# Other durations in a kernel's planner, narrower mask matmuls in the first batch, and rotating tiles handed out by the planner

## Chip, cores, metric

One core of a Trainium2 chip. The metric is the device time of one execution in microseconds; the median of three runs stands for the kernel. A profile of one further execution, with a start and a duration for each instruction, is what the numbers below are read from.

## What is computed

Block-sparse causal attention over four batches of eight heads (768 tokens, head size 64), and then a two-layer feed-forward block with a tanh GELU on the 3072 resulting tokens. In the attention each query sees its own block of 64 keys and those blocks whose mean key scores in the top three.

```python
gate_scores = einsum('bhsd,bhnd->bhsn', q, k.reshape(B,H,12,64,D).mean(3))   # causal blocks only
top_idx = argsort(gate_scores)[..., -3:]
mask = blocks(top_idx | own_block) & causal
attn = softmax(where(mask, 0.125 * q @ k.T, -1e9))
x = (attn @ v).transpose(0, 2, 1, 3).reshape(3072, 512)
out = gelu_tanh(x @ w_in) @ w_out          # 512 -> 2048 -> 512
```

A query in the first three blocks (rows 0 to 191) has at most three causal blocks, so all of them are chosen.

## The kernel before

The work is cut into 16 head pairs `p` (four per batch `b`; `hp` is the place in the batch) and, per batch, a first layer `s1(b)` and a second layer `s2` (`s2_plain(0)` for the first batch; in `s2(b)` of the others 7 half-size products per token tile, with sums formed on VectorE, take the place of 8). While one batch is in its feed-forward part, the pairs of the next are prepared.

**A planner sets the order.** Nothing is issued where it is written. Each piece of work is an `Op` with the engines that it may run on and a duration for each (`add({DVE: 0.56, ACT: 0.84}, ...)` may go to either), the ops that it waits for, a priority, and the buffers it takes and gives back. `Plan.solve` (L53) simulates the engines: of the ops that could start within 0.03 us of the earliest it takes the one with the lowest priority number, and books it on the engine where it would end first. When all are placed, they are issued in order of their planned start (L1226 to L1229). So the given durations decide three things: the order on each engine, which engine gets an op that two could do, and which pooled buffer an op gets. On the chip each engine runs its instructions strictly in the order issued, waiting on semaphores where an input is late: a wrong duration costs only if it makes something early wait behind something late.

**Fillers.** `warm` (L1163) adds 72 matmuls (`NWARM`) of 256 columns at the lowest priority (1e6), whose results nobody reads. The planner puts them wherever it believes TensorE idle, in their order, until they are used up.

**One pair of batch 0** (`pre`, `first` branch): keys and queries are turned by TensorE (`turn`, L391), copied out of PSUM, and the block gate (L512) is a small fp32 matmul; VectorE picks the top three (`sel_e`, L546); TensorE transposes the mask (`mask`, L586). Then `heads2` (L674) goes through six units per pair. For a unit `st_e` (L683) writes the scores of two heads into one of two 1024-column PSUM tiles (`wide`): for each block of columns two matmuls, one per head, of keys by queries, and two that add the mask (`E2` by `mT2`). ScalarE takes exp (`ex_e`, L702), GpSimd cuts the diagonal (`af_e`), TensorE multiplies by the values (`pv_e`, L748), VectorE normalises (`norm2`), TensorE turns the result back (`ot_e`, L808).

**One pair of batches 1 to 3** (`pre`, other branch): VectorE turns keys and queries (`tr`, L414, 0.97 us each) and sums the keys of each block (`ks_all`, L458); the halves are cast to fp16 by VectorE or GpSimd (`kc_all`, L465) and by VectorE or ScalarE (`q16`, L578); gate and choice as above; the mask rows are copied under the queries (`mc`, L627), so that one matmul does scores and mask together (`heads`, L845).

**The feed-forward stage.** `s1(b)` writes 16 units of 8 matmuls into the same two `wide` tiles, each emptied by one GELU on ScalarE (`ge_e`, L949). `s2_plain(0)` is 6 tiles of 16 matmuls, interleaved by the planner with batch 1's attention; each tile is copied out by `cp_e` (L1036) on VectorE or ScalarE. `sums` (L998) and `w_sums` (L980) are the VectorE sums for the later second layers.

**Tiles.** PSUM tiles are pooled by the planner (`takes`, `gives`). Most rotating tiles in the other memory come from pools of the framework, which turn in the order in which the tiles are asked for at issue: loads (`io`, 3 buffers per kind, `iov`, 2), `hd` (3), `hd2` (2), `atp` (6), `obp` (2). In the planner the load buffers are represented by dependences (`free_sd`), others by `last`.

Loads of batches 1 to 3 go out on SyncE's queue in 128-byte rows (`emit_t`, L258); the queue also carries the output stores, in the planned order.

Of the kernel before, what the change touches and what calls it, by code (L numbers as in the profile page):

```python
# [8 lines left out]
FP32 = mybir.dt.float32  # L9
# [123 lines left out]
def kernel(  # L133
# [22 lines left out]
    HALF = S // 2  # L156
    FAST = range(1, B)
# [6 lines left out]
    io = ctx.enter_context(tc.tile_pool(name="io", bufs=PF))  # L164
    iov = ctx.enter_context(tc.tile_pool(name="iov", bufs=PV))
    hd = ctx.enter_context(tc.tile_pool(name="hd", bufs=3))
    hd2 = ctx.enter_context(tc.tile_pool(name="hd2", bufs=2))
    atp = ctx.enter_context(tc.tile_pool(name="atp", bufs=6))
    xtp = ctx.enter_context(tc.tile_pool(name="xtp", bufs=2))
    obp = ctx.enter_context(tc.tile_pool(name="obp", bufs=2))  # L170
# [17 lines left out]

    w_in16 = persist.tile([128, HP, DFF], FP16)
# [23 lines left out]
    for i in range(NB):  # L213
# [8 lines left out]
        "at": ([[x] for x in range(6)], 6), "osb": ([[x] for x in range(2)], 2),  # L222
# [20 lines left out]
    free_sd = {}  # L243

    def load(p, key, held=None, prio=None):
        b, hp = divmod(p, HP)

        def emit(_):
            sd = room.pop(0) if b == 0 and room else (
                iov if key == "v" else io).tile(  # L250
                [128, NC, 2, 64], FP32, tag=key, name=f"{key}_sd_{p}")
            for hh in range(2):
                nc.sync.dma_start(
                    out=sd[:, :, hh, :],
                    in_=SRC[key][b, 2 * hp + hh].rearrange(
                        "(c p) d -> p c d", p=128))
            T[key, p] = sd
        def emit_t(_):  # L258

            sd = io.tile([128, NC * 4, 32], FP32, tag=key, name=f"{key}_sd_{p}")  # L260
            for hh in range(2):
                for a in range(2):
# [7 lines left out]
                 [free_sd.get((key, p - (PV if key == "v" else PF)))  # L270
                  if p - (PV if key == "v" else PF) >= HP else None, held]
                 + moved[-2:-1],
                 prio=10 * p if prio is None else prio)
# [25 lines left out]
    def cast_v(p, old):  # L299
        b, hp = divmod(p, HP)  # L300

        def emit(eng):
            copy(eng, v16[p % NB][:, :, :, 0:64], T["v", p])
        free_sd["v", p] = ld["v16", p] = add(
            {POOL: 0.85}, emit,
            [ld["v", p], old],
            prio=1000 * (b - 1) + 599 + hp if b else 100 * hp - 55)
# [74 lines left out]
    def pre(p):  # L382
# [5 lines left out]
        kcs, ksr, qcs = [], [], []  # L388
        ks = ks16[p % NK]
# [24 lines left out]
        def tr(key):  # L414
            def emit(_):
                T[key + "T32", p] = (hd if key == "q" else hd2).tile(
                    [128, S], FP32, tag=key + "T32", name=f"{key}T32_{p}")
# [5 lines left out]
        if first:  # L423
            for a in range(2):
                t = add({PE: 0.72}, turn("k", a),
                        [ld["k", p] if p else ld["k", 0, a]], pr,
                        takes=("pre", ("wk", p, a)))
                kc = add({DVE: 0.55},
# [3 lines left out]
                def ksb_h(_, a=a):  # L432
                    for x in ([ksb3[p % NK]] if p else
# [11 lines left out]
                        [t, last.get(p - NK, {}).get("gate")], pr - 0.1)  # L445
# [3 lines left out]
                if a == 1:  # L449
                    free_sd["k", p] = t  # L450
            T["ksb", p] = ksb3[p % NK]
        else:
            t = add({DVE: 0.98}, tr("k"),
                    [ld["k", p], last.get(p - 2, {}).get("k32"), sel_3[0]],
                    pr)
            free_sd["k", p] = t
# [6 lines left out]
            ksr.append(add({DVE: 0.93}, ks_all, [t], pr))  # L463
# [9 lines left out]
        def ksb_m(_):  # L473
# [7 lines left out]
                   ksr + [last.get(p - NK, {}).get("gate")], pr))  # L481

        last.setdefault(p, {})["k32"] = add({"NONE": 0.0}, lambda _: None,
                                            kcs + ksr, pr)

        if first:
            def q32():
                if ("qT32", p) not in T:
                    T["qT32", p] = hd.tile([128, S], FP32, tag="qT32",
                                           name=f"qT32_{p}")  # L490
                return T["qT32", p]
            for a in range(2):
                t = add({PE: 0.37}, turn("q", a),
                        [ld["q", p] if p else ld["q", 0, a]], pr,
                        takes=("pre", ("wq", p, a)))
                if a == 1:
                    free_sd["q", p] = t
                qcs.append(add({DVE: 0.55, ACT: 0.49}, turned("q", a, q32),
                               [t, last.get(p - 3, {}).get("pre")], pr,
                               gives=[("wq", p, a)]))  # L500
        else:
            t = add({DVE: 0.98}, tr("q"),
                    [ld["q", p], last.get(p - 3, {}).get("pre")], pr)
            free_sd["q", p] = t
# [4 lines left out]
        for a, (lo, hi) in enumerate(parts):  # L509
# [18 lines left out]
            last.setdefault(p, {})["gate"] = g  # L528

            def gm_e(_, a=a, lo=lo, hi=hi, n=n):  # L530
                if a == 0:
                    T["gx", p] = hd2.tile([128, NC - 1, 32], FP32, tag="gx",
                                          name=f"gx_{p}")
                    T["gm", p] = hd2.tile([128, NC - 1, 2, NBLK], FP32,
                                          tag="gm", name=f"gm_{p}")
                    T["mx8", p] = hd2.tile([128, NG, 8], FP32, tag="mx8",
                                           name=f"mx8_{p}")
                    T["sel", p] = hd2.tile([128, NG, NBLK], FP32, tag="sel",
                                           name=f"sel_{p}")
# [4 lines left out]
                     gives=[("gt", p, a)])  # L544

            def sel_e(_, a=a, lo=lo, hi=hi, n=n):  # L546
# [8 lines left out]
                for x in range(2 * lo, 2 * hi):  # L555
# [9 lines left out]
                      [gx, c_E["gates"], c_E["ones", i]], pr)  # L565
            sels.append(sel)

# [26 lines left out]
        def mask_dma(_):  # L594
            T["mT", p] = hd2.tile([128, S - 128], FP16, tag="mT",
                                 name=f"mT_{p}")
# [4 lines left out]
        if first:  # L601
            mcs = []
            for a, (lo, hi) in enumerate(parts):
                m = add({PE: 0.06 * (hi - lo)},
                        lambda _, a=a, lo=lo, hi=hi: mask(_, a, lo, hi),
                        [sels[a]], pr, takes=("pre", ("mk", p, a)))

# [11 lines left out]
        else:  # L619
# [3 lines left out]
            else:  # L623
                go = add({SP: 1.3}, mask_dma, [sel], -50)
                m = add({"DMA": 0.8}, lambda _: None, [go], pr, lag=6.0)

# [9 lines left out]
            if byPE:  # L636
                add({"NONE": 0.0}, lambda _: None, mcs, pr,
                    gives=[("mk", p, 0)])
            rdy[p] = [kcs[0::2] + [q16s[0], mcs[0], c_E["fill", i]],
                      kcs[1::2] + [q16s[1], mcs[1], c_E["fill", i]]]  # L640
        if p == HP - 1:
            sel_3.append(sel)
        last.setdefault(p, {})["pre"] = add(
            {"NONE": 0.0}, lambda _: None, kcs + q16s + mcs, pr)
# [10 lines left out]
    def table(key, deps, prio):  # L655
        if key not in tables:
            def emit(_):
                t = hd.tile([128, 1], FP32, tag="tab", name="tab_%s_%d" % key)
# [15 lines left out]
    def heads2(p):  # L674
# [3 lines left out]
        for ui, unit in enumerate(units(p)):  # L678
# [4 lines left out]
            def st_e(_, u=u, unit=unit):  # L683
                st = plan.buf[("st",) + u]
                col = 0
                for jc, q0, w in unit:
                    for src, msk in ((kT2[i], False), (E2, True)):
                        mov = mT2[i] if msk else qT2[i]
                        for h in range(2):
                            nc.tensor.matmul(  # L690
                                st[:, 512 * h + col:512 * h + col + w],
                                src[64 * h:64 * h + 64,
                                    jc * 128:jc * 128 + 128],
                                mov[64 * h:64 * h + 64, q0:q0 + w],
                                start=not msk, stop=msk,
# [3 lines left out]
            st = add({PE: n * 2 / 2400 + 0.01}, st_e, rdy[p][late], pr,  # L699
                     takes=("wide", ("st",) + u))  # L700

            def ex_e(_, u=u, n=n):  # L702
                T["at", u] = atp.tile([128, 2, 512], FP16, tag="at",
                                      name="at_%d_%d_%d" % u)
# [5 lines left out]
            ex = add({ACT: 0.17 + 2 * n * 0.000833}, ex_e,  # L710
# [26 lines left out]
            for a in range(2):  # L737
# [21 lines left out]
                pvs[a].append(add({PE: 0.066 * len(cells) + 0.01}, pv_e,  # L759
# [6 lines left out]
        def norm2(a):  # L766
            def emit(_):
                pvv = plan.buf["pv", p, a][:, 0:NC * 66].rearrange(
                    "p (c w) -> p c w", w=66)
                if ("xn", p) not in T:  # L770
                    T["xn", p] = hd.tile([128, NC, 2, 64], FP16, tag="xn",
                                         name=f"xn_{p}")
                zr = hd.tile([128, NC, 1], FP32, tag="zr", name=f"zr_{p}_{a}")
# [7 lines left out]
                     gives=[("pv", p, a)]) for a in range(2)]  # L781
# [478 lines left out]
```

## Time and profile before

| | |
|---|---|
| three runs | 264.86, 265.20, 265.74 us; median 265.2 |
| the profiled execution | 265.39 us, of which 263.7 us from the first to the last instruction |
| TensorE busy, matmuls | 255.0 us (97% of the span) |
| VectorE / ScalarE / GpSimd busy | 180.9 / 162.5 / 83.2 us |
| granted TensorE clock | 0.998 |
| fillers (L1168) | 72, 12.8 us busy |
| first-batch scores (L690) | 192 matmuls |

How to read it: a matmul's recorded duration holds its whole way through the array, while the next one is already fed in. So the time that a stream of matmuls costs is the distance between their starts, and "97% busy" doesn't mean that TensorE ran at its best for 97% of the time. A row of the timeline such as `37.49 0.34 PE L690 ... x2` is a run of two matmuls that began at 37.49 us and whose last result came 0.34 us later. A bracket at the end of a row gives the idle time before it and what ended it.

### The profile page before, as it was taken

The numbers are of one execution on the slowest core, as the hardware profiler recorded it, in microseconds if no ns is written. First come the engines' busy times: TensorE is split into PE (matmuls) and PEld (weight loads), VectorE is DVE, ScalarE is ACT, GpSimd is POOL, SyncE is SP. The second block draws the span as 40 slices with busy tenths as digits, with TensorE's granted clock in tenths as the row PEclk, the third lists the DMA queues.
The fourth block names the chain that finished last, engine by engine and source line by source line (L and its number), as shares of the span: only waits on it lengthen the run. The fifth ranks groups of instructions, "written<-read, shape, count | busy, mean of one in ns | idle before, by whom it ended". The sixth has DMA issues, their size and how long they took to land.

```text
span 263.7 us, 6523 instructions
## 1 busy us (share of the span) xinstructions
PE 255.0 (97%) x2542; PEld 176.8 (67%) x2542; DVE 180.9 (69%) x531; ACT 162.5 (62%) x203; POOL 83.2 (32%) x165
## 2 busy tenths in 40 slices
PE   6999999999998999999989999999999999999994
PEld 5877777565555555555756788665777797666883
DVE  1877745714489999989999999969644463335643
ACT  2368678556968986566887971367799912664000
POOL 8667723002446563221065743100044400000000
PEclk9999999999999999999999999999999999999999
DMA  8998998999798959887896862320104222000222
GB/s 163 218 203 154 159 208 116 176 203 190 155 210 149 206 122 215 173 165 138 154 188 127 160 151 81 104 52 0 27 1 124 50 80 83 0 1 2 80 80 82
DMA packets 130816, 32.63 MB, mean 124 GB/s; under 512 B 124544, under 2 KB 126688, under 8 KB 130784
## 3 DMA queue, kind: packets, MB, share of 16 engines
q1 hardware_dynamic: 126048, 27.62, 51.8%
q0 software_dynamic: 3136, 4.19, 9.9%
q10 hardware_dynamic: 1600, 0.39, 0.8%
q8 instruction: 20, 0.33, 0.5%
q14 instruction: 12, 0.10, 0.1%
HBM read 27.26 MB, written 6.29 MB: 127 GB/s over the span
## 4 chain that ended last, share of the span: by engine, by line
PE 78%; DVE 15%; POOL 2%; ACT 2%; issue 1%; DMA 1%; DVEq 0%; ACTq 0%; POOLq 0%
PE wide L938 27%; PE bank L1070 19%; PE bank L1020 6%; PE wide L866 6%; PE bank L905 4%; PE wide L690 4%; PE bank L1168 3%; DVE XS L1008 3%; PE bank L517 2%; DVE qT L236 2%; PE bank L754 2%; PE bank L398 2%; ACT at L879 1%; DVE mx L556 1%; DVE TS L990 1%; PE bank L401 1%
## 5 line engine op out<-in xcount | busy, mean ns | idle before, releaser
L938 PE MATMUL wide<-xT,w_in 128*128 128x384 f16 x512 | 85.1, 326 | 0.0
L950 ACT ACTIVATE G<-wide 128x768 f16<-128x768 f32 x64 | 51.9, 811 | 47.3 <-PE wide L938 47.3
L938 PEld LDWEIGHTS <-w_in 128*128 128x128 f16 x512 | 49.5, 98 | 33.2 <-issue 1.5
L879 ACT ACTIVATE at<-wide 128x896 f16<-128x896 f32 x72 | 61.3, 916 | 5.9 <-PE wide L866 4.4
L893 POOL TENSOR_SCALAR_AFFINE_SELECT at<-at 128x256 f16<-128x256 f16 x72 | 31.8, 444 | 68.6 <-ACT at L879 68.1
L866 PE MATMUL wide<-qT,kT 76*128 76x512 f16 (+1 forms) x192 | 38.6, 305 | 0.2
L1115 DVE TENSOR_TENSOR osb<-bank,osb 128x512 f32<-128x512 f32 (+1 forms) x36 | 22.3, 620 | 11.6 <-PE bank L1070 11.3
L1070 PEld LDWEIGHTS <-G 128*128 128x128 f16 x288 | 27.3, 98 | 4.2
L905 PEld LDWEIGHTS <-at 128*128 128x128 f16 x504 | 23.6, 97 | 9.2 <-POOL at L893 3.6
L1070 PE MATMUL bank<-w_out,G 128*128 128x256 f16 x216 | 29.6, 272 | 0.0
L905 PE MATMUL bank<-v,at 128*128 128x65 f16 x504 | 26.9, 194 | 1.1 <-DVE xn L794 0.6
L705 ACT ACTIVATE at<-wide 128x1024 f16<-128x1024 f32 (+3 forms) x24 | 21.4, 917 | 9.2 <-PE wide L690 8.0
L1020 PE MATMUL bank<-w_out,G 128*128 128x512 f16 x96 | 26.3, 379 | 0.6 <-DVE xn L794 0.6
L866 PEld LDWEIGHTS <-kT 76*128 76x128 f16 x192 | 15.9, 98 | 10.1 <-issue 1.4
L1070 PEld LDWEIGHTS <-XS 128*128 128x128 f16 x216 | 20.2, 98 | 3.7 <-DVE XS L1008 0.9
L1070 PE MATMUL bank<-TS,XS 128*128 128x256 f16 x144 | 20.3, 273 | 0.5 <-DVE XS L1008 0.5
L1008 DVE TENSOR_TENSOR XS<-G 128x768 f16<-128x768 f16 x12 | 7.3, 607 | 18.5 <-ACT G L950 18.5
L234 POOL CAST v<-v_sd 128x768 f16<-128x768 f32 x13 | 11.7, 899 | 25.6 <-DMA v_sd<-in_v_dram 21.3
L234 POOL CAST kT<-kT 64x768 f16<-64x768 f32 x17 | 14.0, 823 | 16.6 <-DVE kT L418 16.3
L418 DVE STREAM_TRANSPOSE kT<-k_sd 128x768 f32<-128x768 f32 x12 | 11.7, 972 | 6.3 <-DMA k_sd<-in_k_dram 6.2
L1168 PE MATMUL bank<-ident 128*128 128x256 f16 x72 | 12.8, 303 | 2.1 <-DVE ident L180 2.1
L794 DVE TENSOR_TENSOR xn<-bank,zr 128x384 f16<-128x384 f32 x24 | 13.4, 558 | 0.8
(96 smaller groups left out, 325.3 us busy)
## 6 DMA issues: line engine op xcount, KB each, us to landing
out_dram<-osb SPq DMA_DIRECT2D x24, 256.0 KB
v_sd<-in_v_dram SPq DMA_DIRECT2D x26, 192.0 KB
k_sd<-in_k_dram SPq DMA_DIRECT2D x48, 96.0 KB
q_sd<-in_q_dram SPq DMA_DIRECT2D x48, 96.0 KB
w_in<-in_moe_w_in_dram POOLq DMA_DIRECT2D x2, 1024.0 KB, 11.5
w_out<-in_moe_w_out_dram POOLq DMA_DIRECT2D x2, 1024.0 KB, 12.6
G<-in_k_dram SPq DMA_DIRECT2D x4, 192.0 KB
G<-in_q_dram SPq DMA_DIRECT2D x4, 192.0 KB
```

The lines of the kernel that those rows point to most:

```text
L234: nc.gpsimd.tensor_copy(out=out, in_=in_)
L705: nc.scalar.activation(out=T["at", u][:, :, 0:n], in_=plan.buf[("st",) + u].rearrange("p (h w) -> p h w", h=2)[:, :, 0:n], func=AF.Exp, bi ...
L866: nc.tensor.matmul(st[:, x:e], kT16[i][h][0:76, s0:s0 + 128], qT16[i][h][0:76, s0 + (x - cb):s0 + (e - cb)], start=True, stop=True)
L879: nc.scalar.activation(out=T["at", u][:, 0:n], in_=plan.buf[("st",) + u][:, 0:n], func=AF.Exp, bias=0.0, scale=SCALE)
L893: nc.gpsimd.affine_select(out=dg, in_=dg, compare_op=ALU.is_ge, fill=0.0, base=0, pattern=[[0, 2], [1, 128]], channel_multiplier=-1)
L905: nc.tensor.matmul(pvv[:, qc, 0:65], at[:, cb + (qc - jc) * 128: cb + (qc - jc + 1) * 128], v16[i][:, jc, h, :], start=(gi == 0 and jc == ...
L938: nc.tensor.matmul(hps[:, 512 * e:512 * e + HALF], w_in16[:, ci, (2 * j + e) * 128: (2 * j + e + 1) * 128], T["xT", b][:, ci, HALF * h:HAL ...
L950: nc.scalar.activation(out=G[:, :, h, j, :], in_=plan.buf["hps", b, j, h].rearrange("p (e w) -> p e w", e=2)[:, :, 0:HALF], func=AF.Gelu_a ...
L1020: nc.tensor.matmul(plan.buf["ops", b, ti], G[:, f % 2, 2 * ti // NC, f // 2, ti % (NC // 2) * 128:ti % (NC // 2) * 128 + 128], w_out16[:, ...
L1070: nc.tensor.matmul(dst[:, HD * h:HD * h + HD], FACT[m][0][:, j, t * 128:(t + 1) * 128], FACT[m][1][:, j, :], start=(clear and j == 0), sto ...
L1115: nc.vector.tensor_tensor(out=dst(), in0=src(), in1=other(), op=ALU.add)
L1168: nc.tensor.matmul(plan.buf["warm", n][:, 0:256], ident16, z, start=True, stop=True)
```

## The change

- **Durations**: some constants given to the planner are replaced (among others PE: `turn` of q 0.37 to 0.47, a score unit `n*2/2400+0.01` to `cols/2400+0.1`, where `cols` leaves the dropped mask columns out, `pv_e` 0.066 per cell + 0.01 to 0.06 per cell + 0.1, `ot_e` 0.36 to 0.40; ACT: exp of batch 0 0.17 + to 0.13 +; DVE: sums 0.5 and 0.6 to 0.55 and 0.66, joins 0.61 to 0.66; POOL: `af_e` 0.36 to 0.44). Not all of them: a cast of keys by VectorE stays at 0.56.
- **Masks**: in batch 0 the mask matmuls start at query 192 (and 64 columns past the diagonal block's start) where they began with the unit's block of columns.
- **Tiles**: the framework's rotating pools are replaced by fixed tiles in the planner's pools, with the same counts (`zr` now 2), which ops take and give back.
- **Dependences**: some are added for what the pools tracked by themselves (`early`, the GELUs of batch `b-2` before `xT` is written again).
- Priorities are unchanged.

```diff
     plan = Plan({
-        "at": ([[x] for x in range(6)], 6), "osb": ([[x] for x in range(2)], 2),
+        **{kind: ([tuple(persist.tile([128] + dims, dt, name=f"{kind}_{n}_{m}")
+                         for m, (dims, dt) in enumerate(parts))
+                   for n in range(most)], most)
+           for kind, most, parts in (
+               ("at", 6, [([1024], FP16)]),
+               ("osb", 2, [([2, 2, HD], FP32)]),
+               ("ksd", PF, [([NC * 2 * 64], FP32)]),
+               ("qsd", PF, [([NC * 2 * 64], FP32)]),
+               ("vsd", PV, [([NC * 2 * 64], FP32)]),
+               ("k32", 2, [([S], FP32)]), ("q32", 3, [([S], FP32)]),
...
         go = add({SP: 2.4 if dve else 1.15}, emit_t if dve else emit,
-                 [free_sd.get((key, p - (PV if key == "v" else PF)))
-                  if p - (PV if key == "v" else PF) >= HP else None, held]
-                 + moved[-2:-1],
-                 prio=10 * p if prio is None else prio)
+                 [held] + moved[-2:-1],
+                 prio=10 * p if prio is None else prio,
+                 takes=None if inside else (key + "sd", (key + "sd", p)))
...
-                t = add({PE: 0.37}, turn("q", a),
+                t = add({PE: 0.47}, turn("q", a),
...
                 for jc, q0, w in unit:
-                    for src, msk in ((kT2[i], False), (E2, True)):
-                        mov = mT2[i] if msk else qT2[i]
+                    q1 = max(q0, 192, jc * 128 + 64)
+                    for src, mov, lo in ((kT2[i], qT2[i], q0),
+                                         (E2, mT2[i], q1)):
+                        if lo >= q0 + w:
+                            continue
                         for h in range(2):
                             nc.tensor.matmul(
-                                st[:, 512 * h + col:512 * h + col + w],
+                                st[:, 512 * h + col + lo - q0:
+                                   512 * h + col + w],
                                 src[64 * h:64 * h + 64,
                                     jc * 128:jc * 128 + 128],
-                                mov[64 * h:64 * h + 64, q0:q0 + w],
-                                start=not msk, stop=msk,
+                                mov[64 * h:64 * h + 64, lo:q0 + w],
+                                start=mov is qT2[i],
+                                stop=mov is mT2[i] or q1 >= q0 + w,
                                 skip_group_check=True)
                     col += w
-            st = add({PE: n * 2 / 2400 + 0.01}, st_e, rdy[p][late], pr,
+            cols = n + sum(max(0, q0 + w - max(q0, 192, jc * 128 + 64))
+                           for jc, q0, w in unit)
+            st = add({PE: cols / 2400 + 0.1}, st_e, rdy[p][late], pr,
                      takes=("wide", ("st",) + u))
...
-            ex = add({ACT: 0.17 + 2 * n * 0.000833}, ex_e,
+            ex = add({ACT: 0.13 + 2 * n * 0.000833}, ex_e,
...
-                pvs[a].append(add({PE: 0.066 * len(cells) + 0.01}, pv_e,
+                pvs[a].append(add({PE: 0.06 * len(cells) + 0.1}, pv_e,
...
+        if b >= 2:
+            norms = norms + [gelus[b - 2][x] for x in gelus[b - 2]]
...
-                af = add({POOL: 0.36}, af_e, [ex], pr)
+                af = add({POOL: 0.44}, af_e, [ex], pr)
...
-                    {DVE: 0.6}, emit, [w_ready["out", x], prev] + plain.get(x, [])[-1:],
+                    {DVE: 0.66}, emit, [w_ready["out", x], prev] + early + plain.get(x, [])[-1:],
...
-                {DVE: 0.5}, emit, g + [prev, x_free.get((b - 1, m, c))],
+                {DVE: 0.55}, emit, g + [prev, x_free.get((b - 1, m, c))],
```

## Prediction

> **What bounds the kernel.** I read the page's busy times first, then the same by stage, then the timeline of TensorE in each stage for the distance between starts, and the timelines of ScalarE and VectorE beside it. By stage (start and end, length, busy us of each engine with instruction counts, clock, DMA share, GB/s; the next two lines are the same for the fillers alone):
>
> ```profile
> core 0: us, PE busy (x) PEld busy (x) DVE busy (x) ACT busy (x) POOL busy (x), PEclk, DMA share, GB/s
> 12.00:43.00 31.00, 30.93 (x489) 23.10 (x489) 20.11 (x79) 23.70 (x29) 16.80 (x29) 1.00 0.98 176
> 64.00:106.00 42.00, 40.87 (x408) 22.94 (x406) 34.80 (x93) 32.92 (x42) 19.74 (x35) 1.00 0.92 179
> 131.00:142.00 11.00, 9.72 (x123) 6.61 (x121) 10.84 (x23) 8.99 (x11) 6.17 (x12) 1.00 0.96 176
> ...
> 12.00:43.00 31.00, 5.79 (x33) 2.64 (x33) 1.00 0.98 176
> 106.00:131.00 25.00, 1.46 (x14) 1.37 (x14) 1.00 0.85 156
> ```
>
> TensorE bounds nearly everything, at full clock. The stages to look at are batch 0's attention (12 to 43), where no other engine is over 76% busy, and the two in which VectorE is as full as TensorE (64 to 106, 131 to 142). From 142 us on the distances between starts leave under 1 us beyond the gates' own 0.4 each, so nothing is to be had there.
>
> TensorE in the first stage, and a run of 21 small matmuls from later:
>
> ```profile
> 34.88 0.61 PE L1168 MATMUL bank<-ident 128*128 128x256 f16 x4
> 35.43 0.28 PE L690 MATMUL wide<-XS,XS 64*128 64x256 f16 x2
> 35.55 0.27 PE L690 MATMUL wide<-XS,G 64*128 64x256 f16 x2
> ...
> 37.66 0.33 PE L690 MATMUL wide<-XS,G 64*128 64x384 f16 x2
> 37.82 0.22 PE L690 MATMUL wide<-XS,XS 64*128 64x128 f16 x2
> 37.88 0.22 PE L690 MATMUL wide<-XS,G 64*128 64x128 f16 x2
> ...
> 139.15 0.80 PE L905 MATMUL bank<-v,at 128*128 128x65 f16 x21 [0.39 <-DVE xn L794]
> ```
>
> and ScalarE beside it:
>
> ```profile
> 35.05 0.38 ACT L705 ACTIVATE at<-wide 128x256 f16<-128x256 f32 x1 [0.19 <-PE wide L690]
> 36.14 3.08 ACT L705 ACTIVATE at<-wide 128x1024 f16<-128x1024 f32 x3 [0.71 <-PE wide L690]
> ```
>
> ScalarE stood idle 0.71 us for the very scores that came behind four fillers at 34.88: the planner, which books a full unit at 512*2/2400+0.01 = 0.44 us where the two heads' runs take 0.54, believed TensorE idle there. The list of waits has 8.0 us of exps waiting for L690.
>
> **The change, part by part.** Sums are against the profiled execution's own 265.4 us. Where instructions go I take from the order in which they stand on each engine in the two built programs; durations from the rows.
>
> *(a) Masks.* The two heads' matmuls start together, so a mask run costs its distance to the next start: 256 columns 0.11 us (35.43 to 35.55), 128 columns 0.06, 384 columns 0.16. Per pair one run goes from 256 to 64 columns, two from 128 to 64, three from 256 to 192. 192 columns are not in the trace: on the line between 128 and 256, 0.083. 64 columns aren't either: at most the 0.055 of 128, at least the 0.030 of the 65-column run ((0.80-0.19)/20, each with its own weights), which I take, as it is nearest. A pair saves 0.08+2*0.025+3*0.027 = 0.21 us, four pairs 0.85. The Trainium skill speaks against this ("TensorE: Matmul & The Clock Gate", Back-to-back issue gap): in a stream where every matmul has a weight load, it puts 128 columns at about 81 ns. Then 128 to 64 saves nothing and 256 to 64 only 0.03, in sum 0.44 us. The rows decide: 128 columns at 56 ns, 65 at 30, weight loads between them. TensorE is the busy engine here, so I count **-0.85** (between -0.2, if ScalarE limits, and -0.9).
>
> *(b) Fillers.* In batch 0's attention 29 stand where 33 did; before it 23 for 25 (hidden by the first loads, nothing). One costs 0.109 us ((131.06-129.54)/14). **-0.4**, or 0 if the wait is there anyway.
>
> *(c) First layer, batch 0.* One cast of queries (0.82 us on ScalarE, "L232 ACT CAST", mean 823 ns) moves from VectorE to between the third and the fourth GELU. It waits for VectorE's transpose, which ended at 48.3 us, when the third GELU had been done since 47.7. ScalarE has 8*0.1625-0.81 = 0.49 us to spare per unit; 0.6 of waiting and 0.82 of casting exceed it. Between 0 and +0.7; **+0.4**, as part of the stage before is gone too.
>
> *(d) 64 to 106 us.* VectorE here:
>
> ```profile
> 63.95 0.19 DVE L475 TENSOR_TENSOR ksb<-bmask,ks 128x32 f32<-128x32 f32 x1
> 69.15 0.69 DVE L236 COPY osb<-bank 128x512 f32<-128x512 f32 x1 [5.00 <-PE bank L1020]
> 69.76 0.97 DVE L418 STREAM_TRANSPOSE qT<-q_sd 128x768 f32<-128x768 f32 x1
> ```
>
> For 5.0 us it waited in its queue for the first output tile (`cp_e`, tile 0), with the transpose of pair 5's queries behind it. Those were issued by 61.03 us, and the keys before them took 2.7 us from their last issue (58.66) to VectorE's start (61.37), so the queries were there by about 63.7. After the change this copy goes to ScalarE, and transpose, cast and choice of pair 5 come ahead. SyncE gains too: the store of that tile stood at 69.87 ahead of the values of pair 6 and the keys of pair 7, and now stands behind them. Before batch 2's first scores VectorE also loses five query casts (5*0.61) and gains one output copy (0.68): -2.4 us; key casts and mask copies cancel out. What TensorE waits for in this stage, by distances: 0.48 (79.83 to 80.53 for one 0.22 matmul), 0.80 before
>
> ```profile
> 84.87 0.38 PE L1020 MATMUL bank<-w_out,G 128*128 128x512 f16 x1 [0.63 <-DVE xn L794]
> ```
>
> then 0.17, 0.30 and 0.21: 1.96 us, mostly on VectorE. I take two thirds, **-1.3** (0 to -2.0). Against all of it speaks a second rule ("SBUF — State Buffer", Who interferes with whom): a VectorE cast that uses both ports and a GpSimd instruction exclude each other for their whole length. The trace bears it out: VectorE's key cast, alone 0.51 to 0.56 us, took 1.13 at 100.88 while GpSimd cast from 100.77 on. The planner still books 0.56, so some of its new order comes late.
>
> *(e) First layer, batch 1.* Between the fifth and sixth GELU two query casts of pair 10 stand on ScalarE where there was one: 1.65 us against 0.49 to spare, so the sixth GELU ends 1.16+0.81 = 1.97 us after its unit is written, and TensorE wants the tile after 1.30: a wait of 0.67. The planner saw it and put eight fillers there (8*0.109 = 0.87) and a little of the second layer. **+0.9** (0.3 to 1.6, the more the later VectorE is).
>
> *(f) Start of batch 2.* Twelve fillers for fourteen: -0.2. Behind them the waits 0.30, 0.67, 0.25, 0.55, 0.34 = 2.1 us, for exps and VectorE's sums, such as
>
> ```profile
> 134.85 0.39 PE L1070 MATMUL bank<-TS,XS 128*128 128x256 f16 x2 [0.49 <-DVE XS L1008]
> ```
>
> VectorE was without a pause from 115 us to here; now 2.4 us of casts are gone and the 5.0 us idle are used earlier, minus what contention takes back. **-1.4** with the fillers (0 to -2.3).
>
> *Tiles and dependences*: same counts; the loads take buffers freed by the same transposes, the added dependences end long before. Nothing, covered by loads that landed six and more us before VectorE took them (pair 8's keys issued by 80.4, used at 92.2). Two moves in batches 2 and 3 go each way; TensorE runs without gaps there. Nothing. The last output joins are longer only in the plan.
>
> Sum: -0.85-0.4+0.4-1.3+0.9-1.4 = -2.65, so 265.4-2.65 = **262.7 us**. The median of the runs is 0.2 lower than the profiled execution, which I leave within the range.
>
> **Rivals.**
> 1. *ScalarE takes over the first stage.* It was busy 23.7 of 31 us, with two tiles in turn: when one exp follows another at 0.92 us, shorter scores buy nothing. For: three exps in a row without a gap (36.14, 3.08 us). Against: 8.0 us of waits for L690. Then (a) and (b) give 0.2 instead of 1.25: 263.8.
> 2. *Slower: casts on ScalarE in front of GELUs.* Pair 10's transposes stand on VectorE after two choices of 1.7 us and a sum of keys. If VectorE is late there, the sixth GELU waits, then the tile, then TensorE, one for one, and in batch 0 the same at 48 us. Price: (c) 0.7, (e) 0.9 plus the lateness. With (a), (b), (d) and (f) at half, -2.0, it decides from a lateness of 0.4 us on; at 2 us it gives 265.4-2.0+0.7+0.9+2.0 = 267.0. For: casts of up to 1.13 booked at 0.56. Against: 5 us of head start.
> 3. *More.* VectorE's head start removes all waits of (d) and (f): another 0.7+0.7, and (c) is nothing: 260.9.
> 4. *It doesn't do what it says*: the masks are narrower in the built program and the order differs on every engine, so no.
>
> **How the numbers follow.** Forecast 0.60 (its own range 261.5 to 264.2), ScalarE 0.16, slower 0.08, more 0.16. A change of 0.3%, 0.8 us, is about what a measurement of this kernel can tell from none. Faster by more, below 264.4: 0.59 of the forecast, 0.11 of the first rival, all of the third: 0.86. Within: 0.07. Slower: 0.07. Range 260.8 to 264.8.
>
> **What would show it.** (a) first GELU well before 44.1 us, score rows of 64 columns some 30 ns apart; (b) 29 fillers among the scores; (d) no pause of VectorE near 64 to 69 and no TensorE bracket on `xn` near 85; (e) a pause or fillers in the middle of batch 1's first layer; (f) brackets on L1008 gone. Wrong if the first GELU starts at 44 as before, or if TensorE waits for GELUs by more than 2 us in all.

## The result, and the profile after

The changed kernel takes 262.92 us (median of four runs, 262.67 to 263.54) beside 265.03 us before: a ratio of 0.9921, 95% interval 0.9893 to 0.995. Its profiled execution took 262.67 us, of which 261.0 us are the span (before: 265.39 and 263.7). Some executions of the experiments' kernels (two of five in the last one) are longer by some per cent and left out of the comparisons; four of the profiles (both runs with gaps, both with fewer fillers) are of such a one and are called delayed below: TensorE waited 2.94 to 8.09 us in batch 0's first layer for a gate behind late queries, so that stage is not read in them, and in what stands behind it the other engines have had that much of a head start.

Where the 2.73 us of span went is read from the starts of TensorE's matmuls: the first score, the first and the last of the 128 matmuls of each first layer, the end. Lengths in us:

| stretch | before | after | difference | of it, same work moved |
|---|---|---|---|---|
| start to the first score of batch 0 | 11.31 | 10.96 | -0.35 | |
| to the end of batch 0's first layer | 52.87 | 52.05 | -0.82 | |
| to the start of batch 1's | 41.38 | 40.55 | -0.83 | |
| batch 1's first layer | 21.74 | 22.99 | +1.25 | +0.44 |
| to the end of batch 2's | 59.85 | 58.16 | -1.69 | -0.22 |
| to TensorE's end | 72.66 | 72.41 | -0.25 | -0.22 |
| to the end of the span | 3.87 | 3.83 | -0.04 | |

"Moved" are four second-layer matmuls of 0.11 us that now stand within batch 1's first layer, two taken from each of the two stretches behind it (counts of matmuls per stretch: 143 and 155, 580 and 576, 703 and 701, fillers included).

Busy time of the engines by stage, in the same three stages as before (start and end, length, then busy us and instruction counts of each engine, clock, DMA share, GB/s), and the fillers alone in two of their places:

```profile
12.00:43.00 31.00, 30.81 (x491) 23.17 (x488) 20.76 (x80) 24.11 (x32) 17.76 (x30) 1.00 1.00 181
64.00:106.00 42.00, 41.29 (x412) 23.56 (x411) 36.10 (x105) 34.52 (x44) 20.70 (x38) 1.00 0.93 181
131.00:142.00 11.00, 10.91 (x154) 8.36 (x152) 9.96 (x23) 10.77 (x14) 7.03 (x16) 1.00 0.79 139
...
12.00:43.00 31.00, 4.87 (x29) 2.35 (x29) 1.00 1.00 181
104.00:128.00 24.00, 1.20 (x8) 0.78 (x8) 1.00 1.00 164
```

In the last stage TensorE's busy time rose from 9.72 to 10.91 of 11 us: the longest wait left there, by distances between starts, is 0.26 us, where the forecast counted 0.30, 0.67, 0.25, 0.55 and 0.34. The fillers stand as forecast: 29 in the first stage, 8 in the middle of batch 1's first layer.

TensorE's timeline at the same place as before (start, duration, run of matmuls), then ScalarE's:

```profile
33.81 1.05 PE L1200 MATMUL bank<-ident 128*128 128x256 f16 x8
...
34.91 0.19 PE L715 MATMUL wide<-XS,G 64*128 64x64 f16 x2
34.94 0.22 PE L715 MATMUL wide<-XS,XS 64*128 64x128 f16 x2
...
35.25 0.25 PE L715 MATMUL wide<-XS,G 64*128 64x192 f16 x2
35.33 0.27 PE L715 MATMUL wide<-XS,XS 64*128 64x256 f16 x2
```

```profile
35.40 2.85 ACT L734 ACTIVATE at<-wide 128x1024 f16<-128x1024 f32 x3 [0.70 <-PE wide L715]
```

A mask run of 64 columns costs 0.03 us to the next start and one of 192 columns 0.08, as the forecast had them. But ScalarE still stands idle 0.70 us for those scores, and now eight fillers instead of four stand in front of them.

VectorE at the start of batch 1's attention:

```profile
63.09 0.97 DVE L436 STREAM_TRANSPOSE q<-qsd 128x768 f32<-128x768 f32 x1
64.09 0.55 DVE L247 CAST qT<-q 64x768 f16<-64x768 f32 x1
67.60 0.35 DVE L558 STREAM_TRANSPOSE sel<-bank 128x160 f32<-128x160 f32 x1 [2.96 <-PE bank L542]
```

Pair 5's queries are turned at 63.09 and no longer at 69.76, and of the 5.00 us of idling 2.96 are left, now for the gate's matmul: the sign that the forecast gave for its step (d), no pause here, is met in part. The cost is to be seen on ScalarE in batch 1's first layer, and the fillers beside it on TensorE:

```profile
111.11 1.68 ACT L243 CAST qT<-q 64x768 f16<-64x768 f32 x2
112.69 1.51 ACT L985 ACTIVATE G<-wide 128x768 f16<-128x768 f32 x2
```

```profile
111.46 0.48 PE L542 MATMUL bank<-q,ksb 128*32 128x160 f32 x8
111.88 1.48 PE L973 MATMUL wide<-xT,w_in 128*128 128x384 f16 x8
113.19 0.38 PE L1103 MATMUL bank<-w_out,G 128*128 128x256 f16 x2
113.40 0.82 PE L1200 MATMUL bank<-ident 128*128 128x256 f16 x6
```

Two casts, then the GELU 1.1 us late; TensorE fills the time with a gate, two second-layer matmuls and six fillers.

### The profile page after: what moved, and what is told of

It is laid out like the page before. It is cut to its first block, busy times and chain, and to the rows that moved or that the text cites. A ratio compares the mean times of both kernels' runs of the same rounds, so it can differ in the third digit from the quotient of the medians.

```text
span 261.0 us, 6531 instructions
## 1 busy us (share of the span) xinstructions
PE 253.7 (97%) x2542; PEld 176.2 (68%) x2542; DVE 177.8 (68%) x527; ACT 164.4 (63%) x207; POOL 80.8 (31%) x165
## 4 chain that ended last, share of the span: by engine, by line
PE 85%; ACT 6%; DVE 6%; issue 2%; POOL 1%; DVEq 0%; POOLq 0%; ACTq 0%
PE wide L973 32%; PE bank L1103 20%; PE wide L898 7%; PE bank L1055 7%; ACT at L911 5%; PE bank L937 5%; PE bank L1200 3%; PE wide L715 3%; PE bank L542 2%; PE bank L783 2%; PE bank L420 1%; PE bank L417 1%; PE bank L840 1%; PE bank L611 1%; POOL at L925 1%
## 5 line engine op out<-in xcount | busy, mean ns | idle before, releaser
L925 POOL TENSOR_SCALAR_AFFINE_SELECT at<-at 128x256 f16<-128x256 f16 x72 | 29.7, 416 | 64.1 <-ACT at L911 63.3
L1103 PE MATMUL bank<-w_out,G 128*128 128x256 f16 x216 | 30.5, 272 | 0.0
L1055 PE MATMUL bank<-w_out,G 128*128 128x512 f16 x96 | 25.1, 379 | 0.4 <-DVE osb L247 0.4
L245 POOL CAST kT<-k 64x768 f16<-64x768 f32 x17 | 14.4, 845 | 29.1 <-DVE k L436 28.6
L1043 DVE TENSOR_TENSOR XS<-G 128x768 f16<-128x768 f16 x12 | 6.5, 552 | 18.1 <-ACT G L985 18.1
L436 DVE STREAM_TRANSPOSE k<-ksd 128x768 f32<-128x768 f32 x12 | 11.5, 962 | 9.1 <-DMA ksd<-in_k_dram 9.0
L245 POOL CAST v<-vsd 128x768 f16<-128x768 f32 x13 | 11.1, 851 | 18.6 <-DMA vsd<-in_v_dram 18.6
```

What stands on the lines that cost most here:

```text
L245: nc.gpsimd.tensor_copy(out=out, in_=in_)
L925: nc.gpsimd.affine_select(out=dg, in_=dg, compare_op=ALU.is_ge, fill=0.0, base=0, pattern=[[0, 2], [1, 128]], channel_multiplier=-1)
L1055: nc.tensor.matmul(plan.buf["ops", b, ti], G[:, f % 2, 2 * ti // NC, f // 2, ti % (NC // 2) * 128:ti % (NC // 2) * 128 + 128], w_out16[:, ...
L1103: nc.tensor.matmul(dst[:, HD * h:HD * h + HD], FACT[m][0][:, j, t * 128:(t + 1) * 128], FACT[m][1][:, j, :], start=(clear and j == 0), sto ...
```

## The experiments

All ratios are to the kernel before, run on the same chip. The length of the first stage is counted from the first score on, since the first score itself came anywhere from 10.96 to 11.98 us, by the loads. That leaves some play: the order of before needed 30.96 us from there to the first layer in two profiles (its own, and the one with only a copy moved); the order of the change 30.45 in one and, where the first score came 1.02 us later, 30.09 in another (the one with a cast moved in batch 1).

### Parts of the change alone

**Wide masks again**, everything else as after:

```diff
-                    q1 = max(q0, 192, jc * 128 + 64)
+                    q1 = q0
```

> The changed kernel with the mask matmuls at their old widths and nothing else: planned durations, order and buffers stay those of the changed kernel. If TensorE bounds the first stage, as the prediction has it, the first GELU moves from 42.9 to about 43.8 us and the time is 0.85 us longer, about 263.8. If each matmul cost what the rule on streams with weight loads says, +0.44, about 263.4. If ScalarE limits the stage, +0.2, 263.1.

0.9943 [0.9923, 0.9963]. From the first score to the first layer 30.83 us, with the narrow masks 30.45 or 30.09.

**Narrow masks alone**, on the kernel before (its loop with the `q1` of the change, old durations and pools):

> The kernel before with the narrow mask matmuls alone, in its own order. If the masks are worth 0.85 us wherever they stand: the first GELU at 43.2 instead of 44.1 us, 264.2 us. If ScalarE or the planned order takes it up (what TensorE saves, it then waits for the next tile): 264.8 to 265.0.

0.998 [0.9959, 1.0]. Here the stage falls from 30.96 to 30.14 us, by 0.82: all of the 0.85 that TensorE saves. In the new order the gain lies between 0.38 and 0.74. The whole time fell by 0.5 us with an interval of 0 to 1.1, which by itself could not tell 0.85 from 0.2. The rival "ScalarE takes over", which leaves 0.2 for masks and fillers together, is out.

**Old durations** in the changed kernel (tiles and narrow masks stay), and the reverse, **new durations** in the kernel before (old pools, wide masks):

```diff
-            cols = n + sum(...)
-            st = add({PE: cols / 2400 + 0.1}, st_e, rdy[p][late], pr,
+            st = add({PE: n * 2 / 2400 + 0.01}, st_e, rdy[p][late], pr,
...
-                af = add({POOL: 0.44}, af_e, [ex], pr)
+                af = add({POOL: 0.36}, af_e, [ex], pr)
```

> The changed kernel with all planned durations as before: narrow masks and the planner's tiles stay. If the durations bring all but the masks' share, this is the kernel before with narrow masks, about 264.2 us. If the tiles bring it (waits of the framework's pools that the planner didn't know), about 262.9 us, as the changed kernel.

> The kernel before with the new durations alone: wide masks, the framework's pools. If durations bring all but the masks' share: 265.0-1.9 = about 263.1 us. If the tiles do: about 265. If pools of the framework and the new order collide: above 265.

0.9996 [0.9975, 1.0016] and 1.0002 [0.9978, 1.0026]: neither half does anything that can be measured in the whole time (the first although the narrow masks are in it), and together they are worth 0.8%. Stage by stage, the new durations alone already give the 40.55 us between the first two first layers (before 41.38), and take 22.55 us for batch 1's first layer (before 21.74). What is missing is the gain behind it: 59.83 us to the end of batch 2's first layer, as before. The tiles under the old durations don't bring it either: 60.39 us, 0.22 of it moved work.

**All but the tiles** and the dependences added with them (pools of before, new durations, narrow masks):

> The changed kernel with the framework's rotating pools as before: new durations and narrow masks alone. If the tiles and the added dependences are worth nothing in themselves (the prediction's part on tiles): 262.9, give or take 0.5 for another order. If the framework's pools make waits in the new order that the planner doesn't know: 264.4 or more (the fourth experiment less the masks' 0.6).

0.9966 [0.9945, 0.9987]. Again 40.55 and 22.55, and then 59.57 us where the change has 58.16. Of the 1.41 us between them 0.44 are work and fillers that stand elsewhere (below). The rest, 0.97 us, comes with the tiles, which the forecast counted at nothing.

### Why the tiles seem to matter: VectorE keeps GpSimd out

GpSimd and VectorE at the start of batch 2 in the kernel with the new durations alone:

```profile
129.93 0.55 DVE L1008 TENSOR_TENSOR XS<-XS,G 128x768 f16<-128x768 f16 x1
130.40 0.55 DVE L1008 TENSOR_TENSOR G<-G 128x768 f16<-128x768 f16 x1
130.87 0.55 DVE L1008 TENSOR_TENSOR XS<-G,XS 128x768 f16<-128x768 f16 x1
130.90 2.93 POOL L893 TENSOR_SCALAR_AFFINE_SELECT at<-at 128x256 f16<-128x256 f16 x3 [14.52 <-ACT at L879]
131.34 0.55 DVE L1008 TENSOR_TENSOR XS<-G 128x768 f16<-128x768 f16 x1
131.81 0.55 DVE L1008 TENSOR_TENSOR G<-G 128x768 f16<-128x768 f16 x1
132.28 0.55 DVE L1008 TENSOR_TENSOR XS<-XS,G 128x768 f16<-128x768 f16 x1
```

and TensorE there:

```profile
133.15 0.39 PE L905 MATMUL bank<-v,at 128*128 128x65 f16 x7 [1.18 <-POOL at L893]
```

Nine sums, 0.47 us apart without a gap, run from 128.53 to 132.83. The first of the three diagonal cuts in the group began at 130.90 and took 2.20 us, where the median over all 72 is 0.41; it ended only 0.27 us after the row of sums. TensorE waited 1.18 us for it. In the changed kernel the row is broken at this moment by another instruction:

```profile
129.76 0.55 DVE L1043 TENSOR_TENSOR XS<-G 128x768 f16<-128x768 f16 x1
130.11 0.46 POOL L925 TENSOR_SCALAR_AFFINE_SELECT at<-at 128x256 f16<-128x256 f16 x1 [14.13 <-ACT at L911]
130.34 0.74 DVE L247 COPY qT<-mT 12x640 f16<-12x640 f16 x2
```

The test puts something short between the sums, in the kernel with the new durations alone, and then in the one with all but the tiles:

```diff
                                         in1=i1[:, js], op=op)
+                if b == 1:
+                    nc.vector.memset(gap16, 0.0)
```

> The kernel before with the new durations (the fourth experiment), and a small fill of 16 columns on VectorE after each of batch 1's sixteen sums. There a diagonal cut on GpSimd took 2.20 us at 130.9 us instead of 0.40, and TensorE waited 1.34 us for it. If VectorE's unbroken run of sums with two inputs in SBUF kept GpSimd out, the cut takes at most 0.9 us now, TensorE's wait shrinks to 0.3 or less, and the time is 1 us shorter in spite of 16 more instructions: about 264.0. If GpSimd was late for another reason, the cut stays near 2.2 us and the time at 265.0 or a little above.

> All parts but the tiles (new durations and narrow masks on the pools of before, which gave 264.09 us), with a memset of 16 columns on VectorE behind each sum of batch 1, as in the run with the gaps. Theory A, what the rotating tiles were worth is that in their order no unbroken row of two-input sums on VectorE keeps GpSimd out: the diagonal cut of 2.07 us at 130 falls under 0.8, the stretch from the last first-layer matmul of batch 1 to that of batch 2 falls from 59.57 to 58.2 us, and the whole comes to 262.7 us, as fast as the change. Theory B, the tiles give something of their own (buffers that come free in another order): the stretch stays above 59 us and the whole at 263.8 or more.

0.9974 [0.9956, 0.9992] and 0.9958 [0.9938, 0.9978]. The longest cut falls from 2.20 to 0.77 us in the first, and from 2.07 to 0.79 in the second, whose GpSimd and VectorE look so:

```profile
134.59 0.54 DVE L1016 TENSOR_TENSOR XS<-G,XS 128x768 f16<-128x768 f16 x1
...
134.60 1.47 POOL L901 TENSOR_SCALAR_AFFINE_SELECT at<-at 128x256 f16<-128x256 f16 x2 [12.87 <-ACT at L887]
135.07 0.73 DVE L1016 TENSOR_TENSOR XS<-G 128x768 f16<-128x768 f16 x1
```

Each cut gets in at the next gap, and a sum beside it takes 0.73 instead of 0.54. That the row of sums keeps GpSimd out is thereby shown. What it is worth is less sure. The stretch falls from 59.83 to 58.50 us in the first and from 59.57 to 58.66 in the second, but both are delayed profiles; the whole times fell by less, from 265.00 to 264.06 us and from 264.09 to 263.64 in the median of the executions compared (the last on a chip on which the kernel before is 0.15 us slower). The change has 58.16 there with two second-layer matmuls and two fillers fewer (0.44), so 58.60 for the same work: 0.06 from the kernel with gaps. The expected 58.2 had forgotten those 0.44 us. Read so, the tiles give nothing of their own in this stretch, and their order happens to break the row of sums. The whole time doesn't confirm it: the first theory had 262.7 us and the second 263.8 or more, and it came to 263.64, 263.26 at the lowest, between them. The stages, with the change's 21.60 us for the one that isn't read, sum up to a span of 261.3 us, some 263.0 in all; why most executions took longer stays open, and with it whether the tiles, or the dependences, give something of their own.

### The middle terms

**Only the copy of output tile 0 on ScalarE**, in the order of before, which step (d) named as the cause of VectorE's 5.0 us of idling:

```diff
-            op.emit(op.eng)
+            op.emit(ACT if op is T["swap"] else op.eng)
```

> The kernel before in its own order, with one instruction moved: the copy of the first output tile of batch 0 is issued on ScalarE and not on VectorE. If VectorE's 5.0 us of idle time in front of that copy is what makes the stage from 64 to 106 us wait later, as part (d) says: batch 1's first layer starts 0.5 to 0.9 us earlier than 105.6 us, 264.3. If the order of the rest, or the five casts fewer on VectorE, is what counts: 265.0, and the start stays at 105.6.

1.0001 [0.9982, 1.0019], and 41.39 us between the first layers, as before. VectorE there:

```profile
64.18 0.97 DVE L418 STREAM_TRANSPOSE qT<-q_sd 128x768 f32<-128x768 f32 x1
71.33 0.20 DVE L793 RECIPROCAL zr<-bank 128x6 f32<-128x6 f32 x1 [6.18 <-PE bank L905]
71.57 0.56 DVE L794 TENSOR_TENSOR xn<-bank,zr 128x384 f16<-128x384 f32 x1
```

The transpose came 5.6 us earlier, as forecast. But the next in the queue is pair 4's normalisation, and VectorE stood 6.18 us for that: one late thing at the queue's head was replaced by another, with the cast still behind it. The copy alone is not the cause.

**TensorE's durations alone** (the PE constants of the diff, on the kernel before):

> The kernel of before with only the planner's durations for TensorE changed (key turns 0.76, query turns 0.47, scores +0.09 each, sums of heads, joins); those for VectorE, ScalarE and GpSimd stay. With all new durations the stretch from the last first-layer matmul of batch 0 to the first of batch 1 was 40.55 us in every kernel, with the old ones 41.15 to 41.39. Theory A, the order that gains there comes from TensorE's units being booked at what they take: 40.5 to 40.7. Theory B, it comes from the joins and gates of the other engines: 41.1 to 41.4. In both the whole stays at 264.5 to 265.3, as the row of sums early in batch 2 gives it back.

1.003 [1.0015, 1.0044], a little slower than before and, with 265.85 us, above the 265.3 expected at most: the part from the first score to the end of batch 0's first layer took 53.63 us instead of 52.87. Between the first layers 40.90 us: 0.48 of the 0.83. That is between the two theories; by this one profile, more than half of the gain comes from TensorE's units being booked nearer to what they take, and the rest from the other durations. In batch 2 the row of sums strikes here too, with a cut of 2.04 us.

**Pair 10's first query cast on VectorE**, in the changed kernel:

```diff
-            op.emit(op.eng)
+            op.emit(DVE if op is T["swap"] else op.eng)
```

> The change with one instruction moved: the cast of the first head's queries of pair 10, between the fifth and the sixth GELU of batch 1, is issued on VectorE instead of ScalarE; fillers and the two matmuls of the second layer that were put there stay. Theory A (the forecast's step e), two casts on ScalarE make the sixth GELU late and the eight fillers only fill the wait: the fillers now cost what they take, and the first layer of batch 1 still lasts 22.6 to 23.0 us, as fillers and moved work (0.87 and 0.44) are in TensorE's queue; but the pause behind them, if there is one, goes. Theory B, the cast itself is what TensorE stands for beyond the fillers: the stage falls to 22.4 or under. VectorE loses 0.6 us either way, and the whole stays between 262.5 and 263.5 us.

0.9923 [0.9908, 0.9938], and batch 1's first layer takes 22.99 us, to the hundredth as with both casts on ScalarE. The fillers are in TensorE's queue and take their time, wait or no wait.

**No fillers** behind the 23 ahead of the first scores:

```diff
             def emit(_, n=n):
+                if n >= 23:
+                    return
```

> The changed kernel in its own order, with fillers 24 to 72 planned but not issued (the 23 before the first scores stay). If a filler costs its 0.109 us where TensorE is the busy engine, as the prediction counted in its part (b): 49 fewer, 29 in the first stage, up to 3.2 us there and up to 2.2 us around batch 1's first layer and batch 2's start, 257.6 to 260. If fillers stand only where TensorE would wait anyway: 262.9 less 0 to 0.5 us. If TensorE's clock falls without them, longer.

0.9887 [0.9844, 0.993], from 261.38, 261.88 and 263.16 us: some 1.0 us less than the change, neither the full price of 49 fillers (257.6 to 260) nor nothing. From the first score to the first layer 29.27 us instead of 30.45, and batch 1's first layer takes 22.41 instead of 22.99. At the start of batch 2, though, TensorE in this delayed profile has a pause where twelve fillers were. One line of its timeline, and the stages behind it (behind the busy times of the five engines stands the granted clock):

```profile
133.96 0.54 PE L898 MATMUL wide<-qT,kT 76*128 76x512 f16 x2 [1.36 <-ACT at L911]
```

```profile
131.00:134.00 3.00, 1.64 (x16) 1.23 (x15) 2.94 (x8) 2.97 (x5) 0.02 (x1) 1.00 0.94 187
134.00:135.90 1.90, 1.72 (x22) 1.03 (x22) 1.84 (x5) 1.88 (x3) 1.45 (x3) 1.00 0.56 93
135.90:139.30 3.40, 3.40 (x26) 2.25 (x25) 3.37 (x8) 2.37 (x3) 0.98 (x3) 0.50 0.99 159
139.40:145.00 5.60, 5.60 (x79) 4.37 (x77) 4.25 (x9) 5.38 (x7) 4.15 (x9) 1.00 0.29 67
```

The granted clock was 0.50 for 3.4 us, from 135.9 us on, and the stretch to the end of batch 2's first layer took 59.69 us instead of 58.16. But the kernel doesn't do this every time. Half the clock for 3.4 us is a loss of 1.7 us, 0.0065 of the span; the mean granted clock was 0.992 in the execution of 263.16 us, but 0.999 in the other two, which leaves no room for it. Nor does a pause of this length always bring it: the kernel with all but the tiles stood as long at the same place, and kept its clock.

```profile
132.28 0.39 PE L912 MATMUL bank<-v,at 128*128 128x65 f16 x7 [1.38 <-POOL at L900]
```

```profile
134.00:140.00 6.00, 6.00 (x82) 4.57 (x79) 5.52 (x12) 5.68 (x9) 4.77 (x9) 1.00 0.92 153
```

What else it takes for the clock to fall is not shown.

**Fillers only where they might guard the clock**: the change without the 29 and the 8, with the last 12, and with the cast above on VectorE.

```diff
             def emit(_, n=n):
+                if 23 <= n < 60:
+                    return
```

> The change without the 29 fillers of the first stage and the 8 in batch 1's first layer, and with pair 10's first query cast on VectorE; the 12 fillers at the start of batch 2 stay. Without any of the fillers the first stage came to an end 0.64 us earlier and batch 1's first layer took 22.41 us instead of 22.99, but TensorE then stood 1.36 us at the start of batch 2, and the granted clock was 0.61 between 137 and 140 us, so that the stretch to the end of batch 2's first layer took 59.69 us instead of 58.16. Theory A, the last twelve fillers guard the clock and the others only take room: the first layer of batch 0 starts at 40.8, batch 1's takes 22.1 to 22.4, the stretch behind it 58.2 to 58.7 at clock 1.0, and the whole comes to 261.4 to 262.0 us, faster than the change. Theory B, what is won ahead of batch 2 is waited for there, since VectorE's sums end when they did: the stretch takes 59 us and more and the whole is at 262.6 or above. Theory C, the first stage's fillers guard its clock too: the granted clock between 11 and 41 us falls under 1.0 and the whole is above 263.

0.987 [0.9849, 0.9891], with 261.35, 262.09 and 262.53 us: faster than the change. Two more executions took 271.15 and 272.40 us; the profile is of the first of these, a delayed one. Its stages:

```profile
11.00:41.00 30.00, 28.21 (x473) 21.49 (x473) 20.47 (x88) 23.43 (x30) 16.48 (x29) 1.00 1.00 182
...
135.00:140.00 5.00, 4.76 (x44) 3.40 (x42) 4.91 (x11) 4.58 (x6) 1.19 (x2) 1.00 0.93 172
140.00:150.00 10.00, 10.00 (x143) 7.58 (x141) 9.84 (x23) 9.90 (x13) 6.88 (x14) 1.00 0.75 137
```

The first layer of batch 0 starts at 40.77 us at full clock, batch 1's takes 22.25 us, and the stretch behind it 58.15 at clock 1.00, as the first theory has it; the last two come after a wait of 8.09 us. By the whole times the kernel can't be told from the version with no fillers at all (the intervals overlap), of which two executions kept their clock. So the 29 and the 8 fillers only take room, but that the other twelve guard the clock is not shown, nor, with two long executions in five, that this version is the better one to use.

## Why the prediction was right, and where its steps were not

The forecast was 262.7 us, by a sum of -2.65; the span fell by 2.73. The direction and the bound (TensorE nearly everywhere) were right, and most terms were near, three of them for another reason than the one given. That the sums agree to 0.1 us is luck: 0.35 of the 2.73 is the start, which no term foresaw, the terms (b), (c) and (d) were off by 0.2 to 0.5 us and made up for one another in part, and the medians of the runs lie only 2.11 us apart (by the interval 1.3 to 2.8).

- **(a) masks, -0.85.** The runs cost 0.03 and 0.08 us as taken from the nearest rows, and the price of about 81 ns for 128 columns that the prediction quotes is not what these runs show (0.06). Of the 0.85, 0.82 reaches the stage in the old order and 0.4 to 0.7 in the new. The first GELU starts at 42.91 us and no longer at 44.08.
- **(b) fillers, -0.4.** Mis-sized. All 29 of them cost 1.18 us (30.45 to 29.27; 0.8 to 1.3 by the other profiles of the two orders), so 0.03 to 0.045 each and not 0.109: the rest of their time falls where TensorE would have stood anyway. By that price four fewer are worth 0.1 to 0.2, an estimate.
- **(c) cast before a GELU, +0.4.** Wrong. The cast waited for nothing: the third GELU ended, the cast began, the fourth followed at 47.25 us.

```profile
45.68 0.81 ACT L985 ACTIVATE G<-wide 128x768 f16<-128x768 f32 x1 [0.49 <-PE wide L973]
46.52 0.83 ACT L243 CAST qT<-q 64x768 f16<-64x768 f32 x1
47.25 0.80 ACT L985 ACTIVATE G<-wide 128x768 f16<-128x768 f32 x1
```

  The forecast kept VectorE's transpose at its old time of 48.3 us, though VectorE comes to it earlier too, and left out that the gate's matmuls on TensorE (0.4 us) put the next unit later. TensorE has no start distance above that of its work in this layer, before or after. Together (a) to (c) were forecast at -0.85 and came to -0.82; another -0.35 is the start, which differs that much between executions.
- **(d) 64 to 106 us, -1.3.** Measured -0.83, and the step that failed is "for 5.0 us it waited in its queue for the first output tile": true, but taking that one away alone gave nothing. Of TensorE's waits, counted by distances between starts as in the forecast, 1.21 of the 1.96 us are left: 0.38, 0.31 and 0.52 behind the matmuls at 81.2, 84.0 and 85.3 us. With the first output copy alone on ScalarE they were all still there. So the term was too large and its cause was wrong: the new order takes 0.75 us of them and not two thirds. VectorE's casts of keys went from 0.79 to 0.69 us in the mean, so the contention that was weighed against this step took less than before. What it is in the order that saves the 0.75 stays open beyond the share of TensorE's durations.
- **(e) batch 1's first layer, +0.9.** Measured +0.81 beyond the moved work, but not as a wait of 0.67 that fillers hide: without fillers the layer takes 22.41 us, which is the old 21.74, 0.44 of moved work and 0.23 of waiting. The eight fillers make the other 0.58 us. The forecast's wait of 0.67 did not take off the gate and the second-layer matmuls that cover most of it.
- **(f) start of batch 2, -1.4.** Measured -1.69 less 0.22 of moved work, so -1.47. The brackets on the sums are gone. By the forecast's count, the waits of 2.1 us there have shrunk to 0.8. But the cause given, casts taken off VectorE, holds only where no row of sums keeps GpSimd out: with the new durations alone this stretch gained 0.02.
- **Tiles, nothing.** Wrong by about 1 us in batch 2 under the new durations. The runs with gaps suggest that it is their order that does it and nothing of their own, but do not show it. And not all loads were six us early, as the forecast had it: before the change VectorE waited 6.22 us for the keys of pair 5, and in the last experiment's profile 9.06 us for queries, where TensorE then stood.

```profile
61.37 0.98 DVE L418 STREAM_TRANSPOSE kT<-k_sd 128x768 f32<-128x768 f32 x1 [6.22 <-DMA k_sd<-in_k_dram]
```

- **The tail, nothing:** two matmuls moved ahead, -0.22, and 0.03.

The rival "slower by casts" failed because the casts cost TensorE no more than 0.23 us in batch 1's first layer and nothing that can be seen in batch 0's.

## What to carry to other kernels

In a planned schedule the terms don't add up part by part: here two halves of a change are worth nothing each that can be measured, as one of them makes a collision that is gone when both stand together, so look at the order that comes out at each place before crediting a part. A wait at the head of an in-order queue is worth something only if the next entry behind it is not late itself. Fillers in TensorE's queue are not free: here one cost 0.03 to 0.07 us of its 0.109, and leaving out 49 of them gained about 1 us. Keep only those that a run shows to be needed, and look at several executions, as one profile can show a fall of the clock that the others don't have.

## What the runs showed of the hardware

- A row of two-input fp16 sums on VectorE, 0.47 us apart, kept a 0.41 us instruction of GpSimd from ending for 2.20 us (2.04 and 2.07 in two other kernels); a memset of 0.07 us between the sums brought the longest to 0.77 to 0.79, with the sum beside it at 0.73 instead of 0.54. Why it does so the runs don't show, only that the row is what keeps GpSimd waiting.
- A pause of 1.36 us of TensorE was followed, 2 us after its end, by a granted clock of 0.50 for 3.4 us; one of 1.38 us in another kernel was not, nor were those of 1.18 and 1.13 in two others. In the delayed profiles, pauses of 2.94 and 3.34 us were followed by 3.4 us at 0.50, and within those of 6.54 and 8.09 us began 6.8 us at 0.50.
- A run of mask matmuls (two heads side by side, a weight load each) of 64 columns took 0.03 us from start to start, one of 192 columns 0.08.
